# Two-part cache loads into any two free slots, and slots handed out in the order they came free

## The chip, the cores and the metric

The kernel runs on one core of one Trainium2 chip. Its time is the time on the device, in microseconds, of one execution; lower is better. The core has five engines with instruction streams of their own: TensorE (PE in the profile, its weight loads PEld), VectorE (DVE), ScalarE (ACT), GpSimd (POOL) and SyncE (SP). In this kernel SyncE issues the loads, and 16 DMA engines carry them out.

## The reference

The program is four layers for 8 sequences with one new token each: an attention layer A over cached keys and values, an MLP layer B, then A and B once more with the same weights and the same caches.

```python
def _A_ref(x, k_cache, v_cache, wq, wo):            # caches: 8 x 8 heads x 4096 x 256, bf16
    q = (x @ wq).reshape(B, Sq, 16, 256).transpose(0, 2, 1, 3)
    k = jnp.repeat(k_cache, 2, axis=1)
    v = jnp.repeat(v_cache, 2, axis=1)
    scores = jnp.einsum("bhqd,bhkd->bhqk", q, k) * (256 ** -0.5)
    p = softmax(scores)
    o = jnp.einsum("bhqk,bhkd->bhqd", p, v)
    return o.transpose(0, 2, 1, 3).reshape(B, Sq, 16 * 256) @ wo

def _B_ref(x, w1, w2, w3, w4):                      # one token: the shifted parts are zero
    ...
    x1 = x + hs
    return x1 + gelu(layernorm(x1) @ w3) @ w4

x = x + _A_ref(layernorm(x), A_k_cache, A_v_cache, A_wq, A_wo)
x = x + _B_ref(layernorm(x), B_w1, B_w2, B_w3, B_w4)
x = x + _A_ref(layernorm(x), A_k_cache, A_v_cache, A_wq, A_wo)
x = x + _B_ref(layernorm(x), B_w1, B_w2, B_w3, B_w4)
```

The four shifted pieces of `hs` move tokens by one or two places. With one token each of them is empty, so `hs` is zero and `w1` and `w2` don't matter. The large data are the two caches, read for both attention layers.

## The kernel before

A **unit** is one head of one sequence in one of the two attention passes, `(pass, sequence, head)`: 2 x 8 x 8 = 128 units. The keys and the values of a unit are 2 MiB each and are cut into four **parts** of 512 KiB. In each of 128 partitions a part is 4 KB, and the four parts of a partition are neighbours in memory: parts 0 and 1 together are one run of 8 KB per partition, and so are parts 2 and 3.

The parts live in 31 **slots** of 4 KB per partition, which are cut from one large tile, `slab` (L79, L80). A key part passes through two slots: it is loaded raw into one, VectorE transposes it into another (L554), and the raw slot is free again. TensorE uses the transposed keys for the scores (`k_part`, matmuls at L645). A value part is loaded into a slot and used where it lies (`v_part`, matmuls at L622). The transposed keys of six of the eight heads of a sequence stay in their slots from the first pass to the second (a few of these parts are parked in PSUM meanwhile and copied back at L512), so that they are loaded only once. Loaded are 832 parts.

The order of the work is written out by hand. The main loop (L784) goes over units, in four steps each. In a step come, among others, transposes for a part ahead, the scores of one part (`k_part`), the softmax pieces of the unit before, and the value parts planned for this step (`v_part`). Between the first and the second pass of a sequence lies the MLP, a chain of small steps on TensorE, VectorE and ScalarE (`mid_steps`); the loop fills it with units of other sequences. Below, this stretch is the layer change. `loads` is the list of all loads in the order in which they are to be issued.

The slots are managed in the same walk, on the host, when the program is made. `free` is the list of free slots. Each time the walk reaches an instruction that ends the use of a slot, the slot is put at the end of `free`, and `pump` (L502) issues as many loads as it can, always keeping one free slot back (`RESERVE`, L18), which a transpose can take as its destination (L550). On the chip, a load into a slot waits until the instruction that freed it has run; that wait follows from the slot that was chosen. SyncE issues the loads in order, each one behind the one before it, so a load that waits holds up those behind it. A load also waits for the one eight places before it, since eight completion semaphores go round.

`wide` (L453) holds the parts that may be loaded two at a time: those whose loads are planned outside the layer changes. For them `take_two` (L479) looks for an even slot and its neighbour, both free, and the load is one transfer of 1 MiB, one run of 8 KB per partition on both sides. If there is no such pair and at least `ENOUGH` = 7 parts are under way, `pump` stops and waits for a pair (L522); with fewer under way it loads one part. `take` (L472) prefers a slot whose neighbour is not free, so that pairs stay whole, and the lowest number among those. One part is a transfer of 512 KiB, one run of 4 KB per partition.

Of the kernel before, what the change touches and what calls it, by code (L numbers as in the profile page):

```python
# [15 lines left out]
UNIT = 2048  # L16
N_SLOTS = 31
RESERVE = 1  # L18
# [11 lines left out]
def kernel(  # L30
# [48 lines left out]
    slab = slotp.tile([128, N_SLOTS * UNIT], BF16, name="slab")  # L79
# [291 lines left out]
    lone = {b: [(1, b + 2, g) for g in loose] for b in range(4)}  # L371
# [31 lines left out]
    t = 0  # L403
    while t < n_units:
# [4 lines left out]
        p, b, g = units[t]  # L409
        n = 1  # L410
# [3 lines left out]
        for j in range(parts_):  # L414
            m = n // parts_ + (j < n % parts_)
# [26 lines left out]
    for t in order:  # L442
        for s in range(4):
            i = late_v.get((t, s), 4 * t + s + LAG)
            if t in ends or units[t + 1 : t + 2] == [GAP]:
                i = 4 * t + (6, 6, 7, 7)[s]
            elif t + 1 == n_units:
                i = 4 * t + (5, 5, 6, 7)[s]
# [7 lines left out]
    for i in range(4 * n_units + 8):  # L456
        n = len(loads)
# [6 lines left out]
        t, q = divmod(i + 2, 4)  # L464
# [3 lines left out]
    free = list(range(N_SLOTS))  # L468
# [2 lines left out]

    def take():  # L472

        lone = [x for x in free if x ^ 1 not in free]
        x = min(lone or free)
        free.remove(x)
        return x

    def take_two():  # L479

        both = [x for x in free if x % 2 == 0 and x + 1 in free]
        if both:
            free.remove(both[0])
            free.remove(both[0] + 1)
        return both[:1]

    extra = []
    for c in range(3):
# [13 lines left out]
    def pump():  # L502
        while loads and len(free) > RESERVE:
            kind, t, i = loads[-1]
            _, b, g = units[t]
            if kind == "p":
                loads.pop()
                x = take()
                dst = slots[x].rearrange("p (e q c x) -> p q c e x", e=4, q=2, c=4)
                for j in range(2):  # L510
                    src = park[parked[g, i]][j][:].bitcast(BF16)
                    nc.scalar.copy(dst[:, j], src.rearrange("p (c e x) -> p c e x", c=4, e=4))  # L512
                kt_of[(1, b, g), i] = x
                continue
            cache, of = (A_k_cache, raw_of) if kind == "k" else (A_v_cache, v_of)
            n, two = 1, (kind, t, i + 1)
            if i % 2 == 0 and two in wide and two in loads[-PAIR_VIEW:]:
                x = take_two() if len(free) > RESERVE + 1 else []
                if x:
                    n, x = 2, x[0]  # L520
                    loads.remove(two)
                elif under_way[0] >= ENOUGH:  # L522
                    return
            loads.pop()
            if n == 1:
                x = take()
            src = cache[b, g].rearrange("(p s e) d -> p s (e d)", s=4, e=8)
            nc.sync.dma_start(
                slab[:, UNIT * x : UNIT * (x + n)].rearrange("p (s d) -> p s d", s=n),
                src[:, i : i + n],  # L530
            )
            for m in range(n):
                of[t, i + m] = x + m
            under_way[0] += n
            n_loads[0] += n
            if n_loads[0] >= 8 and extra:
                nc.sync.dma_start(*extra.pop(0))
# [3 lines left out]
    def transposes(i):  # L541


        while len(parts) - len(todo) < by[i]:
            t, s = todo[-1]
            if 4 * t + s > i and ((t, s) not in raw_of or not free):
                return
            todo.pop()
            raw = raw_of.pop((t, s))
            kt = kt_of[units[t], s] = take()  # L550
            src = slots[raw].bitcast(FP32).rearrange("p (q c e i) -> p q c e i", q=2, c=4, e=4)
            dst = slots[kt].bitcast(FP32).rearrange("p (e q c r) -> p q c e r", e=4, q=2, c=4)
            for q in range(2):
                nc.vector.transpose(dst[:, q], src[:, q])  # L554
            _, b, g = units[t]
            if (g, s) in parked:
                for q in range(2):
                    dst = park[parked[g, s]][q][:].rearrange("p (c e r) -> p c e r", c=4, e=4)
                    nc.vector.transpose(dst, src[:, q])
            free.append(raw)  # L560
            under_way[0] -= 1
            pump()
# [49 lines left out]
    def v_part(t, s):  # L612
        if s == 0:
            at = PO + 4 * (nth[t] % n_po)
            pos[t] = pyb[:, at : at + 4].rearrange("p (k h) -> p k h", h=2)
            if nth[t] == n_po // 2:
                nc.vector.memset(pyb[:, PO : PO + 4 * (len(order) - n_po)], 0.0)
        v = v_of.pop((t, s))
        vv = slots[v].rearrange("p (c d) -> p c d", d=Dh)
        for c in range(8):  # L620
            for k in range(2):
                nc.tensor.matmul(  # L622
                    pos[t][:, k, :],
                    vv[:, c, 128 * k : 128 * k + 128],
                    pts[t][:, 8 * s + c, :],
                    start=(t == 0 and s == 0 and c == 0 and k == 0),
                    stop=True,
                    skip_group_check=True,
                )
        free.append(v)  # L630
        under_way[0] -= 1
        pump()

    def k_part(t, s):
        u = units[t]
        p, b, g = u
        if s == 0:
            assert t not in runs or t in ready
            scs[t] = scb[t % 2][:, 0:64].rearrange("p (c b h) -> p c b h", b=4, h=2)
        key = (u if fresh(u, s) else (1, b, g)), s  # L640
        ktv = slots[kt_of[key]].rearrange("p (e c m x) -> p e c m x", e=4, c=2, x=2)
        for c in range(2):
            for db in range(4):
                for x in range(2):
                    nc.tensor.matmul(  # L645
                        scs[t][:, 2 * s + c, :, :],
                        ktv[:, db, c, :, x],
                        Qblk[run_of[t][0]][:, run_of[t][1], db, x, :, :],
                        start=(db == 0 and x == 0),
                        stop=(db == 3 and x == 1),  # L650
                    )
        if p == 2 or g in loose or (g, s) in parked:
            free.append(kt_of.pop(key))
            pump()
# [129 lines left out]
    for t in range(n_units + 1):  # L784
        cur = t < n_units
        for q in range(4):
            i = 4 * t + q
# [152 lines left out]
```

## Time and profile before

| | before |
|---|---|
| median of 3 runs | 1124.85 us (1121.68 to 1127.41) |
| the profiled execution | 1124.39 us, span 1122.6 us |
| granted TensorE clock | 1.000 |
| read from HBM | 446.77 MB, 398 GB/s over the span |
| loads of two parts | 155 of values, 109 of keys |
| loads of one part | 202 of values, 102 of keys |
| from issue to landing, two parts | 12.6 us (values), 12.9 us (keys), median |
| from issue to landing, one part | 8.0 us (values), 8.6 us (keys), median |

The span runs from the first to the last instruction of the profiled execution; its own time is 1.8 us longer than its span. Where the profile cuts the span into 40 slices, one slice is 28 us. GB/s is what the DMA engines moved in a slice, and the DMA digits say how busy they were in tenths. In the lines on waits, an arrow points from who waited to what released it; the numbers are microseconds in total, how often, and the longest. SPq stands for SyncE's queue of DMA issues.

### The profile page before, as it was taken

How to read it: one execution, taken by the hardware profiler on the slowest of the kernel's cores; microseconds unless marked ns; L12 is line 12 of the kernel's file. 1: busy time of each engine (PE TensorE's matmuls, PEld its weight loads, DVE VectorE, ACT ScalarE, POOL GpSimd, SP SyncE). 2: the span in 40 equal slices, each digit the busy share in tenths (PEclk: the TensorE clock that was granted, in tenths of full speed). 3: DMA queues.
4: the chain of work that ended last, by engine and by line, in shares of the span. 5: the costliest groups of instructions: out<-in, count | busy, mean ns of one | idle time of the engine just before them, and what ended most of it. 6: DMA issues, size and time to landing. Idle time of an engine off the chain costs nothing. (4 is left out here: it accounts for less than half of the span.)

```text
span 1122.6 us, 46232 instructions
## 1 busy us (share of the span) xinstructions
PE 684.8 (61%) x20737; PEld 640.8 (57%) x20737; DVE 549.3 (49%) x1305; ACT 306.8 (27%) x1360; POOL 104.2 (9%) x156
## 2 busy tenths in 40 slices
PE   3345675666656575665756676666666665565765
PEld 2334564566646575655646565555656665565765
DVE  4347544644455445554546534653456425554322
ACT  1112223321332212421233222422243222421241
POOL 0000000100000000100001001000001000100101
DMA  9999999999999999999999999999999999999992
GB/s 366 396 419 425 405 409 424 423 418 389 392 425 423 411 402 420 424 423 395 418 403 424 412 412 388 425 423 413 363 417 424 422 402 374 424 422 411 363 403 93
DMA packets 89174, 449.76 MB, mean 401 GB/s; under 512 B 9344, under 2 KB 15376, under 8 KB 54800
## 3 DMA queue, kind: packets, MB, share of 16 engines
q1 hardware_dynamic: 88976, 446.81, 98.0%
q8 instruction: 162, 2.65, 0.8%
q14 instruction: 36, 0.29, 0.1%
HBM read 446.77 MB, written 0.01 MB: 398 GB/s over the span
## 5 line engine op out<-in xcount | busy, mean ns | idle before, releaser
L554 DVE STREAM_TRANSPOSE slab<-slab 128x512 f32<-128x512 f32 x640 | 413.4, 686 | 217.0 <-DMA slab<-in_A_k_cache_dram 158.1
L622 PEld LDWEIGHTS <-slab 128*128 128x128 bf16 x8192 | 273.5, 106 | 296.9 <-DMA slab<-in_A_v_cache_dram 245.5
L622 PE MATMUL bank<-pt,slab 128*128 128x2 bf16 x7168 | 259.9, 166 | 246.0 <-DMA slab<-in_A_v_cache_dram 174.7
L645 PE MATMUL bank<-Qblk,slab 128*128 128x8 bf16 x8192 | 296.9, 168 | 71.3 <-DVE slab L554 40.0
L645 PEld LDWEIGHTS <-slab 128*128 128x128 bf16 x8192 | 268.0, 105 | 78.7 <-DVE slab L554 47.4
L681 ACT ACTIVATE pe<-bank,small 128x32 bf16<-128x32 f32 x256 | 61.3, 296 | 417.1 <-DVE small L678 417.1
L723 POOL TENSOR_TENSOR small<-small 128x2 f32<-128x2 f32 x112 | 78.2, 698 | 794.1 <-DVE small L719 794.1
L712 ACT CAST pt<-bank 32x64 bf16<-32x64 f32 x448 | 91.1, 203 | 100.6 <-PE bank L704 96.1
L678 DVE TENSOR_REDUCE small<-bank 128x2 f32<-128x256 f32 x128 | 54.1, 423 | 103.3 <-PE bank L668 103.0
L719 DVE TENSOR_REDUCE small<-bank 128x2 f32<-128x64 f32 x128 | 27.2, 212 | 124.9 <-ACT pt L712 106.4
L164 ACT CAST Qblk<-bank 32x32 bf16<-32x32 f32 (+1 forms) x272 | 48.4, 178 | 121.2 <-PE bank L158 118.9
L668 PE MATMUL bank<-rows,small 128*128 128x128 bf16 x256 | 48.5, 293 | 19.0 <-DVE small L660 18.8
L660 DVE TENSOR_REDUCE small<-bank 128x2 bf16<-128x64 f32 x128 | 26.4, 206 | 59.6 <-PE bank L645 59.4
L622 PE MATMUL bank<-pt_far,slab 128*128 128x2 bf16 x1024 | 36.9, 166 | 25.0 <-DMA slab<-in_A_v_cache_dram 24.3
L704 PE MATMUL bank<-pe,rows 128*128 128x64 bf16 x512 | 51.2, 241 | 0.5 <-issue 0.5
L704 PEld LDWEIGHTS <-rows 128*128 128x128 bf16 x512 | 33.7, 124 | 27.8 <-issue 27.5
L694 PE MATMUL bank<-pe,small 128*128 128x64 bf16 x128 | 27.3, 213 | 33.4 <-ACT pe L681 32.0
L180 PEld LDWEIGHTS <-wo_sb 128*128 128x128 bf16 x1152 | 35.5, 104 | 8.6 <-issue 7.5
L180 PE MATMUL bank<-OT,wo_sb 128*128 128x1 bf16 x1024 | 33.2, 165 | 5.5 <-ACT OT L591 4.5
L135 PEld LDWEIGHTS <-wq_sb 128*128 128x128 bf16 x864 | 30.6, 106 | 9.2 <-issue 4.7
L512 ACT COPY slab<-park 128x1024 bf16<-128x1024 bf16 x32 | 30.4, 1024 | 8.2 <-DVE slab L554 6.1
L591 ACT ACTIVATE OT<-bank,small 128x2 bf16<-128x2 f32 x122 | 25.5, 261 | 23.9 <-PE bank L622 22.5
(113 smaller groups left out, 386.4 us busy)
## 6 DMA issues: line engine op xcount, KB each, us to landing
slab<-in_A_v_cache_dram SPq DMA_DIRECT2D x155, 1024.0 KB, 12.6
slab<-in_A_k_cache_dram SPq DMA_DIRECT2D x109, 1024.0 KB, 12.9
slab<-in_A_v_cache_dram SPq DMA_DIRECT2D x202, 512.0 KB, 8.0
slab<-in_A_k_cache_dram SPq DMA_DIRECT2D x102, 512.0 KB, 8.6
wo_sb<-in_A_wo_dram SPq DMA_DIRECT2D x4, 896.0 KB, 11.3
wq_sb<-in_A_wq_dram SPq DMA_DIRECT2D x3, 1024.0 KB, 6.8
w_sb<-in_B_w_dram SPq DMA_DIRECT2D x1, 1568.0 KB, 12.4
w_sb<-in_B_w_dram SPq DMA_DIRECT2D x3, 448.0 KB, 16.8
```

Source lines behind the costliest of these rows:

```text
L135: nc.tensor.matmul(pv[:, i, j, :], cols(big[:, c, :], m + i * half), rows[:, c, :], start=(i == 0 and j == 0 and c == 0), stop=True, skip_ ...
L164: nc.scalar.copy(dst, src)
L180: nc.tensor.matmul(y[:, c, :], chunk(wo_sb[:, k, :], c), o[:, k, :], start=False, stop=True, skip_group_check=True,)
L554: nc.vector.transpose(dst[:, q], src[:, q])
L622: nc.tensor.matmul(pos[t][:, k, :], vv[:, c, 128 * k : 128 * k + 128], pts[t][:, 8 * s + c, :], start=(t == 0 and s == 0 and c == 0 and k ...
L645: nc.tensor.matmul(scs[t][:, 2 * s + c, :, :], ktv[:, db, c, :, x], Qblk[run_of[t][0]][:, run_of[t][1], db, x, :, :], start=(db == 0 and x ...
L668: nc.tensor.matmul(mzs[t][:, 128 * h : 128 * h + 128], pm[:, h : h + 1].to_broadcast([128, 128]), ident, start=True, stop=True,)
L678: nc.vector.tensor_reduce(nm, mx, AX.X, ALU.max, negate=True)
L681: nc.scalar.activation(pe[:].rearrange("p c b h -> p h (c b)")[:, h], scs[t].rearrange("p c b h -> p h (c b)")[:, h], ACT.Exp, bias=nm[:, ...
L704: nc.tensor.matmul(pp[:, c], sel, pe[:], start=True, stop=True)
L712: nc.scalar.copy(pts[t][sl].rearrange("p (k c) h -> p k c h", c=4), pp[sl, :, :, pb, :].rearrange("p c k h -> p k c h"),)
L723: nc.gpsimd.tensor_tensor(out=rz_of[t], in0=zs, in1=mone, op=ALU.pow)
```

## The change

A load of two parts takes the two slots that have been free longest, whichever they are, in place of an even slot and its neighbour. The load's destination has three dimensions: partitions, the two slots with the step between them, and the 4 KB in a slot. Where the two slots happen to be neighbours, it is one run of 8 KB as before. `take` hands out the slot that has been free longest. The rule that `pump` stops when it gets no two slots and 7 parts are under way stays, and so does the reserve of one slot; what is loaded, in which order, and which loads may be of two parts is unchanged. Since slots are chosen differently, the points at which loads stand among the other instructions shift, and with them how many loads are of two parts: 297 in place of 264, with 238 of one part in place of 304.

```diff
     def take():
 
-        lone = [x for x in free if x ^ 1 not in free]
-        x = min(lone or free)
-        free.remove(x)
-        return x
+        return free.pop(0)
 
     def take_two():
 
-        both = [x for x in free if x % 2 == 0 and x + 1 in free]
-        if both:
-            free.remove(both[0])
-            free.remove(both[0] + 1)
-        return both[:1]
+        two = sorted(free[:2])
+        del free[:2]
+        return two
...
             if i % 2 == 0 and two in wide and two in loads[-PAIR_VIEW:]:
-                x = take_two() if len(free) > RESERVE + 1 else []
-                if x:
-                    n, x = 2, x[0]
+                xs = take_two() if len(free) > RESERVE + 1 else []
+                if xs:
+                    n = 2
                     loads.remove(two)
                 elif under_way[0] >= ENOUGH:
                     return
             loads.pop()
             if n == 1:
-                x = take()
+                xs = [take()]
             src = cache[b, g].rearrange("(p s e) d -> p s (e d)", s=4, e=8)
             nc.sync.dma_start(
-                slab[:, UNIT * x : UNIT * (x + n)].rearrange("p (s d) -> p s d", s=n),
+                slab.rearrange("p (x d) -> p x d", d=UNIT)[:, xs[0] : xs[-1] + 1 : max(xs[-1] - xs[0], 1)],
                 src[:, i : i + n],
             )
             for m in range(n):
-                of[t, i + m] = x + m
+                of[t, i + m] = xs[m]
```

## The prediction

> **What bounds the kernel now.** I read the page from the top: busy times, the forty slices, the DMA queues.
>
> ```profile
> PE 684.8 (61%) x20737; PEld 640.8 (57%) x20737; DVE 549.3 (49%) x1305; ACT 306.8 (27%) x1360; POOL 104.2 (9%) x156
> ...
> DMA  9999999999999999999999999999999999999992
> GB/s 366 396 419 425 405 409 424 423 418 389 392 425 423 411 402 420 424 423 395 418 403 424 412 412 388 425 423 413 363 417 424 422 402 374 424 422 411 363 403 93
> ...
> q1 hardware_dynamic: 88976, 446.81, 98.0%
> ```
>
> No engine is above 61%. The 16 DMA engines are busy at 98%, and the bytes are fixed by the problem. So two things can move the time: how fast a busy DMA engine moves bytes, and how often it has nothing to do. The GB/s line shows both: stretches at 424, and dips to 363.
>
> For the first I asked for the DMA view of two stretches of 20 us: 340 to 360, where only two-part loads run, and 650 to 670, where only one-part loads run. First 340 to 360, then 650 to 670:
>
> ```profile
> DMA packets 1162, 8.48 MB, mean 424 GB/s; under 512 B 130, under 2 KB 130, under 8 KB 130
> ...
> q1 hardware_dynamic: 1158, 8.42, 100.2%
> ```
> ```profile
> DMA packets 2273, 8.31 MB, mean 415 GB/s; under 512 B 252, under 2 KB 252, under 8 KB 2270
> ...
> q1 hardware_dynamic: 2270, 8.27, 101.7%
> ```
>
> Both stretches are full. A two-part load into neighbouring slots is one run of 8 KB in each partition and travels as 8 KB packets; a one-part load travels as 4 KB packets. Each queue packet under 512 B is the end mark of a load. So 1158 - 130 = 1028 packets of 8 KB took 20 us x 16 engines, 311 ns each; 2270 - 252 = 2018 packets of 4 KB took 158.6 ns each, 317.1 ns for a pair.
>
> For the second, the stretches in which the DMA moves clearly less (columns: stretch, length, busy time of the five engines with instruction counts, granted clock, DMA share, GB/s):
>
> ```profile
> 240.00:280.00 40.00, 25.42 (x760) 23.71 (x760) 18.68 (x55) 6.90 (x33) 3.21 (x5) 1.00 1.01 395
> 300.00:320.00 20.00, 10.15 (x311) 9.03 (x309) 8.05 (x17) 5.95 (x22) 1.39 (x2) 1.00 1.01 396
> 380.00:400.00 20.00, 12.30 (x357) 11.65 (x354) 6.95 (x20) 4.49 (x22) 1.40 (x2) 1.00 1.01 390
> 500.00:540.00 40.00, 26.11 (x812) 24.62 (x810) 17.83 (x48) 8.09 (x39) 2.79 (x4) 1.00 1.00 402
> 560.00:580.00 20.00, 11.69 (x354) 10.76 (x354) 10.37 (x22) 5.89 (x30) 2.10 (x3) 1.00 1.02 396
> 640.00:660.00 20.00, 12.03 (x380) 11.31 (x376) 6.90 (x17) 4.49 (x22) 1.40 (x2) 1.00 1.01 397
> 680.00:700.00 20.00, 11.12 (x350) 10.54 (x346) 10.39 (x22) 4.86 (x24) 1.40 (x2) 1.00 0.99 376
> 780.00:820.00 40.00, 26.72 (x824) 25.59 (x825) 16.61 (x51) 8.19 (x39) 3.34 (x5) 1.00 0.98 373
> 920.00:940.00 20.00, 13.74 (x437) 13.24 (x435) 9.28 (x21) 6.11 (x30) 1.95 (x3) 1.00 0.97 349
> ```
>
> Against the 415 of full 4 KB traffic they lack, as length x (1 - GB/s / 415): 1.9, 0.9, 1.2, 1.3, 0.9, 0.9, 1.9, 4.0 and 3.2 us, 16.2 us in all. They lie around the change from one layer to the next, where most slots hold keys that wait for the second pass.
>
> What the loads wait for there is in SyncE's own waits:
>
> ```profile
> SPq L528 <- PE bank L622: 241.9, 187, 5.3
> SPq L528 <- DVE slab L554: 162.9, 75, 5.9
> ```
>
> L622 (a V part's matmuls) and L554 (a transpose) are what frees slots: the loads queue behind the freeing of slots.
>
> Last, the chain of waits at its end (start, length, what):
>
> ```profile
> 1021.67 8.09 DMA slab<-in_A_v_cache_dram
> ...
> 1032.87 4.68 DMA slab<-in_A_v_cache_dram
> 1037.63 0.54 issue
> ...
> 1108.35 0.86 PE bank L622 x32
> ```
>
> Up to 1037 us the end waits for loads. After that, 85 us of matmuls, softmax and MLP follow with no load in the chain: a faster or slower DMA there changes nothing.
>
> **The change, term by term.** The profiled execution took 1124.39 us (span 1122.6), 0.46 below the median of 1124.85; I add to 1124.4.
>
> 1. *Smaller packets.* Counted in the two built programs: before, 264 two-part loads, all in neighbouring slots, and 304 of one part; after, 297 of two parts, of which 36 happen to get neighbouring slots, and 238 of one. The 261 others have two runs of 4 KB in each partition. Slab packets before: 128 x (264 + 304) = 72,704. After: 128 x (36 + 238) + 256 x 261 = 101,888. That is 29,184 more, 1,824 on each engine. A load written in two separate runs is not in the trace; the nearest row is the stretch at 650, where a pair of 4 KB packets took 317.1 - 311.3 = 5.9 ns longer than one of 8 KB: 10.8 us. Low end: that stretch also has 122 more end marks, which a two-part load wouldn't; at their recorded 9 ns (packet records) they are 0.34% of it, which leaves 4.8 ns and 8.8 us. High end: the packet records themselves, 159 and 309 ns, so 9 ns and 16.4 us. I take 10.8, a sustained rate, since the recorded durations of neighbouring packets overlap (share 101.7%). Of the 264 two-part loads, 15 are issued after 1037 us, where the chain has no load: x 0.94 gives **+10.2 us** (8.2 to 15.4). No cover hides it: the DMA is full.
>
> The Trainium skill, "DMA: Bandwidth & Descriptors", Specifications, gives 512 B as the smallest transfer for line rate; by that, 4 KB and 8 KB pieces are equally fast and this term is zero. The trace disagrees: 415 against 424 GB/s in two full stretches. The same page (Why small descriptors are slow) speaks of about 3 cycles of overhead per packet; at the 850 MHz that it gives for the fabric that is an estimate of 3.5 ns, 6.4 us for the 1,824 packets.
>
> 2. *Fewer loads.* 33 fewer issues and end marks: 33 x 9 ns = 0.3 us on each engine, left out. An issue with more runs can cost SyncE more (L537: 984 ns median for the 1,024 runs of a wo load, 328 ns for a plain one); at 256 runs an estimate of 0.5 us. SyncE spends over 700 us waiting for slots, so this is hidden except behind an empty queue.
>
> 3. *Loads wait for an older slot.* One free slot is always kept back. Counted in the order that the planner writes out: before, 435 of 568 loads write a slot freed by the very event that let the load be issued (78 of 125 in the layer changes); after, 15 of 535 (0 of 119), since the oldest free slot goes first and the kept one is the newest. So a load is ready one freeing earlier, as if one more part were queued. Where the DMA is full this buys nothing. In a dip it fills up to one part's time, 524,288 B at 415 GB/s = 1.26 us. Capped so, the nine dips give 1.26 + 0.9 + 1.2 + 1.26 + 0.9 + 0.9 + 1.26 + 1.26 + 1.26 = 10.2 us, times 78/125 = **-6.3 us**. Ends: 0, if what empties the queue is that nothing is freed for longer; -16.2, if the dips vanish. I take the capped sum: it follows from one slot.
>
> 4. *No holding out for neighbours.* Before, up to 8 slots lie free while a load waits for a pair (2.5 free on average after a load, 1.4 after the change). This happens outside the layer changes, where the stretch at 340 is full anyway: 0. Just behind a layer change it may add to term 3, within its end.
>
> 5. *A new wait on VectorE.* The slot kept back is what a transpose takes as its destination. Before, 51 of 256 transposed parts took one that a V part's matmuls (L622) had just freed; after, 194. VectorE then waits for TensorE, and behind the transpose are queued its softmax maxima, sums and MLP steps, for which TensorE and ScalarE wait. Nearest row:
>
> ```profile
> DVE slab L554 <- PE bank L622: 11.3, 8, 2.8
> ```
>
> 11.3 us over 51 such parts is 0.22 us a part; 143 more make 32 us. VectorE is idle for half the span, so it counts only near the dips: the nine stretches are 240 of 1037 us, 7.3 us; even there the DMA lacks only 16 of 240 us. Ends 0 and 7.3; I take **+2 us**, nearer to zero for that reason.
>
> Sum: 1124.4 + 10.2 - 6.3 + 2 = 1130.3, so **1130 us**, 0.5% above the median.
>
> **Rivals.**
> - *The dips were the whole price.* One more queued part, and the slots no longer held out for pairs behind the layer changes, close all dips (-16.2), term 5 stays 0 and term 1 is at its low end: 1124.4 + 8.2 - 16.2 = 1116 us, faster. For it: SyncE's 163 us behind transposes. Against it: the deepest dips (4.0 and 3.2 us) are longer than one part. It decides once terms 3 and 5 together return over 15.4 us against 10.2.
> - *The wait moves to VectorE.* If each of the 143 new waits lasts the 1.4 us that the 8 seen ones last, they are 202 us, 23% of it in the dips' stretches, 46 us; if a quarter reaches the DMA, +11.6 in place of +2: 1140 us. For it: at a layer change TensorE and VectorE already wait for one another. Against it: TensorE is idle for 39% and usually done early.
> - *Splitting is free* (a two-run load travels like an 8 KB one; the skill's 512 B rule points that way): 1124.4 - 6.3 + 2 = 1120 us. Against it: the two full stretches.
>
> **How the numbers follow.** About 0.5% (1119.2 to 1130.5) is what a measurement of this kernel can tell from no change. The forecast case has 0.58; its ends put 0.28 within 0.5% and 0.30 above. The first rival has 0.17 (faster), the second 0.17 (slower), free splitting 0.08 (0.05 same, 0.03 faster). So faster 0.20, same 0.33, slower 0.47. The range must take in 1116 and 1140 but for 2 in 10: 1118 to 1141, the top also for term 1 at 15.4 without any refund (1142). The forecast's own range is 1124 to 1138.
>
> **What would show it.** Term 1: packets under 8 KB rise by 58,368 (128 x 238 + 256 x 261 - 128 x 304) less some 500 end marks, to about 112,600, packets of 8 KB fall to about 5,000, and full stretches run at 415 to 418 where they ran at 424. If full stretches stay at 424, splitting is free. Term 3: SyncE's waits for L622 and L554 shrink, and the nine dips are shallower by about 1 us each; unchanged dips prove it wrong. Term 5: VectorE's wait for L622 at the transposes rises from 11 us to some 40; far above 100 speaks for the second rival. The tail behind the last load in the chain stays near 85 us; if it changes by several us, my split at 1037 us is wrong.

## The result, and the profile after

The changed kernel takes 1919.75 us (median, 1917.46 to 1927.82) against 1123.26 us before: 1.71 times as long, 95% interval 1.7044 to 1.7155. The forecast was 1130 us. The loss is 796 us, nearly eighty times the largest single term that I had worked out.

The first lines of the page after (busy times, the slices, the packets, the DMA queue):

```profile
PE 683.5 (36%) x20737; PEld 645.1 (34%) x20737; DVE 552.6 (29%) x1305; ACT 306.8 (16%) x1360; POOL 104.4 (5%) x156
...
DMA  9745965668655785557965487646765586545962
GB/s 378 282 133 167 352 252 199 219 239 336 242 176 177 263 333 197 177 177 252 348 230 183 155 337 280 221 156 233 299 215 202 189 344 236 198 154 191 360 243 68
DMA packets 117831, 449.77 MB, mean 235 GB/s; under 512 B 8816, under 2 KB 14848, under 8 KB 112640
...
q1 hardware_dynamic: 117632, 446.81, 64.9%
```

The engines do the same work as before, and the packets are the ones forecast: 112,640 under 8 KB (forecast about 112,600) and 5,191 larger ones. But the DMA engines, busy at 98% before, are busy at 65%. No packet became slower: in the packet records a 4 KB packet took 159 ns before and after. Between the packets the DMA engines now stand idle. The dips are no longer the layer changes: the stretches with two-part loads, 424 GB/s before, are the slow ones, most of them at 133 to 250, and the layer changes, where loads have one part, stand out at 330 to 360.

What stands still shows best at the score matmuls. They read transposed keys, which VectorE writes, not a load. This is what ended TensorE's idle time (matmuls and weight loads) ahead of them, first before (L645), then after (the same line, now L640); columns: us in total, times.

```profile
  DVE slab L554: 87.4, 123
  issue: 54.2, 54
```
```profile
  DMA slab<-in_A_v_cache_dram: 924.4, 157
  DMA slab<-in_A_k_cache_dram: 553.9, 92
  issue: 342.0, 55
  DVE slab L549: 186.4, 90
```

Before, no idle time ahead of a score matmul was ended by a load. After, most of it is, and mostly by loads of *values*, which the scores never read. (Matmuls and weight loads wait side by side, so these sums count much of the time twice; ahead of the matmuls alone TensorE stood idle for 996 us.) The transposes, which read keys, wait for loads of values too, first before, then after:

```profile
DVE slab L554 <- DMA slab<-in_A_v_cache_dram: 3.8, 2, 2.1
```
```profile
DVE slab L549 <- DMA slab<-in_A_v_cache_dram: 224.4, 43, 9.4
```

A piece of the timeline after shows the rhythm (start, length, engine, line, what; in brackets the idle time before it and who ended it):

```profile
164.17 0.57 PE L640 MATMUL bank<-Qblk,slab 128*128 128x8 bf16 x16 [4.68 <-DMA slab<-in_A_k_cache_dram]
...
166.71 0.37 SPq L523 DMA_DIRECT2D slab<-in_A_v_cache_dram  x1
171.93 0.51 PEld L640 LDWEIGHTS <-slab 128*128 128x128 bf16 x16 [6.64 <-issue]
171.96 0.57 PE L640 MATMUL bank<-Qblk,slab 128*128 128x8 bf16 x16 [6.59 <-DMA slab<-in_A_v_cache_dram]
...
172.56 0.37 SPq L523 DMA_DIRECT2D slab<-in_A_k_cache_dram  x1
...
177.67 2.65 DVE L549 STREAM_TRANSPOSE slab<-slab 128x512 f32<-128x512 f32 x4 [3.65 <-DMA slab<-in_A_k_cache_dram]
...
177.71 0.57 PE L640 MATMUL bank<-Qblk,slab 128*128 128x8 bf16 x16 [4.49 <-DMA slab<-in_A_k_cache_dram]
...
180.38 0.37 SPq L523 DMA_DIRECT2D slab<-in_A_v_cache_dram  x1
```

One load of 1 MiB is issued, it lands about 5 us later, the score matmuls and transposes that waited for it run, and only then is the next one issued. Here the loads have lost their queue. The waits of SyncE and the time to landing say the same:

```profile
SPq L523 <- DVE slab L549: 1034.8, 219, 13.9
SPq L523 <- PE bank L617: 145.1, 102, 9.2
```
```profile
slab<-in_A_v_cache_dram SPq DMA_DIRECT2D x169, 1024.0 KB, 5.5
slab<-in_A_k_cache_dram SPq DMA_DIRECT2D x128, 1024.0 KB, 5.6
```

A two-part load lands in 5.5 us, where it took 12.6 in the full queue before: the load itself is not slow, it is alone. The issues at 166.7, 172.6 and 180.4 us make two loads of 1 MiB in 13.7 us, 153 GB/s.

The waits of the built program say why. I took each wait of an engine for a load and compared the slots that the load writes with those that the waiting instruction uses. Before, every such wait is for a load that writes one of them. After, 232 waits of the score matmuls and 235 of the transposes, 467 in all, are for a load that writes none of the slots in use, and in each of them a slot in use lies between the two slots of the load. The other way there are fewer: 33 loads wait for an instruction of TensorE or VectorE that uses none of their slots, but one between them. So SyncE waits for a transpose nearly always on account of the load's own slot, and the transpose is late because it waits for an earlier load. The waits are set when the program is made, and by these counts a load written with a step is taken there to write the whole stretch from its first slot to its last.

### The profile page after: what moved, and what is told of

It is laid out like the page before. It is cut to its first block, busy times and chain, and to the rows that moved or that the text cites. A ratio compares the mean times of both kernels' runs of the same rounds, so it can differ in the third digit from the quotient of the medians.

```text
span 1915.4 us, 46423 instructions
## 1 busy us (share of the span) xinstructions
PE 683.5 (36%) x20737; PEld 645.1 (34%) x20737; DVE 552.6 (29%) x1305; ACT 306.8 (16%) x1360; POOL 104.4 (5%) x156
## 2 busy tenths in 40 slices
DMA packets 117831, 449.77 MB, mean 235 GB/s; under 512 B 8816, under 2 KB 14848, under 8 KB 112640
## 5 line engine op out<-in xcount | busy, mean ns | idle before, releaser
L640 PE MATMUL bank<-Qblk,slab 128*128 128x8 bf16 x8192 | 295.6, 168 | 996.4 <-DMA slab<-in_A_v_cache_dram 544.9
L640 PEld LDWEIGHTS <-slab 128*128 128x128 bf16 x8192 | 264.7, 105 | 1015.0 <-DMA slab<-in_A_v_cache_dram 379.5
L663 PEld LDWEIGHTS <-small 128*128 128x128 bf16 x256 | 16.8, 106 | 56.8 <-DVE small L655 56.4
```

Of the source, the lines that this page charges most:

```text
L640: nc.tensor.matmul(scs[t][:, 2 * s + c, :, :], ktv[:, db, c, :, x], Qblk[run_of[t][0]][:, run_of[t][1], db, x, :, :], start=(db == 0 and x ...
L663: nc.tensor.matmul(mzs[t][:, 128 * h : 128 * h + 128], pm[:, h : h + 1].to_broadcast([128, 128]), ident, start=True, stop=True,)
```

## The experiments

**Theory 1, false waits:** whatever uses a slot between the two slots of a load waits for that load, and the load for it. **Theory 2, the order of handing out:** transposes get the newest slot and wait for TensorE (the second rival of the prediction). **Theory 3:** a load with a step is slow in the DMA engines.

### Two loads in place of one with a step

The changed kernel with this edit:

```diff
-            nc.sync.dma_start(
-                slab.rearrange("p (x d) -> p x d", d=UNIT)[:, xs[0] : xs[-1] + 1 : max(xs[-1] - xs[0], 1)],
-                src[:, i : i + n],
-            )
+            if xs[-1] - xs[0] > 1:
+                for m in range(2):
+                    nc.sync.dma_start(slots[xs[m]], src[:, i + m])
+            else:
+                nc.sync.dma_start(
+                    slab[:, UNIT * xs[0] : UNIT * (xs[0] + n)].rearrange("p (s d) -> p s d", s=n),
+                    src[:, i : i + n],
+                )
```

> The slots, their order and the order of the work are those of the changed kernel; only, a load of two parts whose slots are not neighbours is issued as two loads of one part, so that no load has a step (36 loads of two parts in neighbouring slots stay, 760 loads of one part). Theory 1, false waits: a load with a step is taken to write everything from its first slot to its last, so what uses the slots between waits for it, and it for them. Then nearly all of the 800 us goes: 1115 to 1145 us (before, plus up to 16 us for 4 KB packets, less up to 10 for older slots). Theory 2, the order in which slots are handed out (transposes get the newest slot and wait for TensorE): it stays above 1800 us. Theory 3, a load with a step is slow in the DMA engines: 1115 to 1145 us as well, with the loads landing as fast as plain ones; the run with gapped pairs tells 1 from 3.

Measured: 1125.84 us against 1125.07, ratio 1.0011 (1.0000 to 1.0022). The slots, their order and the order of the work are those of the changed kernel, and the whole loss is gone. Theory 2 falls. In its program no wait of an engine is for a load that doesn't write a slot in use.

### Pairs with an unused gap

With the 31st slot given up for room, an unused gap is put between the two slots of each pair. The slots, the order and the waits stay; only each two-part load has a step, with nothing used in between. The control is the kernel before with `N_SLOTS = 30`.

```diff
-    slab = slotp.tile([128, N_SLOTS * UNIT], BF16, name="slab")
-    slots = [slab[:, UNIT * i : UNIT * i + UNIT] for i in range(N_SLOTS)]
+    slab = slotp.tile([128, N_SLOTS * UNIT + (N_SLOTS // 2 + 1) * GAP_COLS], BF16, name="slab")
+    at_of = [UNIT * i + (i + 1) // 2 * GAP_COLS for i in range(N_SLOTS)]
+    slots = [slab[:, a : a + UNIT] for a in at_of]
...
-                slab[:, UNIT * x : UNIT * (x + n)].rearrange("p (s d) -> p s d", s=n),
-                src[:, i : i + n],
+                slots[x]
+                if n == 1
+                else slab[:, at_of[x] : at_of[x] + 2 * (UNIT + GAP_COLS)].rearrange(
+                    "p (s d) -> p s d", s=2
+                )[:, :, 0:UNIT],
+                src[:, i] if n == 1 else src[:, i : i + 2],
```

> The kernel before with 30 slots in place of 31: the control for the run with gapped pairs, which needs the room. One slot less means one part less in flight around the layer changes; by the prediction's third term this costs about what one more slot would give back, up to 10 us: 1123 to 1140 us.

> The control with 30 slots and an unused gap of 32 bytes between the two slots of each pair: the same slots, order and waits, but each of the 246 loads of two parts is written in two separate runs of 4 KB, with nothing that is used between them. Theory 1: no false waits, so only the packet term is left, 246 x 8 packets on each engine at 5 to 9 ns: 10 to 18 us above the control. Theory 3: the load with a step is slow in itself, hundreds of us above the control.

> As the run with gapped pairs (30 slots, 246 loads of two parts in two runs each), but the unused gap is 256 bytes in place of 32, so that every slot starts at a multiple of 256 bytes, as in the kernel before. The 32-byte gap cost 28 us, of which the packet term explains 10 to 18. If the rest came from the shifted starts of the slots (a quarter of the 4 KB packets took 164 ns or more there, 159 in the other runs), this run is 5 to 18 us above the control with 30 slots: 1130 to 1144 us, packets at 159 ns and full stretches at 415 GB/s or more. If it came from the load with a step as such, it stays at 1148 to 1156 us.

Measured: the control 1125.45 us (1.0006, 0.9991 to 1.0021), so one slot less costs nothing that can be told. With a gap of 32 bytes (`GAP_COLS = 16`) 1153.67 us (1.0252, 1.0226 to 1.0277), with 256 bytes (`GAP_COLS = 128`) 1135.57 us (1.0086, 1.0066 to 1.0106). The GB/s in the slices, first with 32, then with 256 bytes:

```profile
GB/s 353 386 407 410 381 409 410 410 404 374 403 410 409 397 380 391 409 410 389 405 401 410 410 393 385 412 408 399 389 407 408 407 382 377 408 407 391 357 411 94
```
```profile
GB/s 354 391 411 419 386 417 417 418 412 386 414 417 417 403 394 417 418 417 390 408 408 418 418 396 368 417 417 416 392 415 418 418 384 391 417 417 391 382 417 87
```

A full stretch moves 417 where two-part loads with a step run over a gap of 256 bytes, against 424 for neighbours. So 246 loads with a step and no false waits cost 1135.57 - 1125.45 = 10.1 us, the packet term. (The two ran on different chips; by their ratios to the kernel before, 1.0086 and 1.0006, it is 9.0 us.) Theory 3 falls: steps cost about 10 us, not 800. These steps span 4 KB and a gap, and in the changed kernel two slots lie up to 27 others apart, but its 4 KB packets took the same 159 ns. The first gap cost 28 us, outside its expected 10 to 18. The other 18 us belong to the shifted slots; more on that at the end.

### One slot between, and the nearest two of three

The kernel before, with pairs made of a slot and the next but one:

```diff
-        lone = [x for x in free if x ^ 1 not in free]
+        lone = [x for x in free if x ^ 2 not in free]
...
-        both = [x for x in free if x % 2 == 0 and x + 1 in free]
+        both = [x for x in free if x % 4 < 2 and x + 2 in free]
...
-                slab[:, UNIT * x : UNIT * (x + n)].rearrange("p (s d) -> p s d", s=n),
+                slab.rearrange("p (x d) -> p x d", d=UNIT)[:, x : x + 2 * n - 1 : 2],
```

> The kernel before with its own handing out, but a pair is a slot and the next but one, so each of its 256 loads of two parts has a step and exactly one slot lies between its two. In the program, 97 waits of other engines then name a load that does not touch the slots they use (in the changed kernel 467, in the kernel before none). Theory 1: a clear loss but a fraction of the 800 us; in proportion to these waits 800 x 97 / 467 = 165 us, 1290 us, range 1160 to 1450. Theory 2: no loss beyond the packets, 1123 to 1145 us. Theory 3: 256 of 261 such loads are there, so about the whole loss, 1800 us or more.

Measured: 1395.39 us (1.2407, 1.2382 to 1.2431). Its handing out is that of before, and one slot between two is enough for 270 us, inside the range that was expected of theory 1. What held up its score matmuls (L645), as above:

```profile
  DMA slab<-in_A_v_cache_dram: 349.8, 48
  DVE slab L554: 157.6, 102
  DMA slab<-in_A_k_cache_dram: 59.5, 8
```

The loads are there again as releasers, for 409 us in place of 1478. The changed kernel with less distance between the two slots:

```diff
-        two = sorted(free[:2])
-        del free[:2]
-        return two
+        two = min(((a, b) for a in free[:3] for b in free[:3] if a < b), key=lambda p: p[1] - p[0])
+        for x in two:
+            free.remove(x)
+        return list(two)
```

> The changed kernel, but a load of two parts takes those two of the three slots longest free that lie nearest to each other (lone slots by age as before; 91 loads get neighbours, 206 have a step). Counted in the program, 282 waits of the score matmuls and the transposes name a load that writes none of the slots they use; counted alike, the changed kernel has 467 and the run with one slot between 153 (the number 97 in that run's expectation left out 57 at the transposes). If the loss goes with these waits, 796 us x 282 / 467 = 481 us: 1600 us, range 1480 to 1720. If it goes with the number of loads with a step (206 against 261 and 256), 1750 or, by the run with one slot between, 1340.

Measured: 1483.5 us (1.3165, 1.3122 to 1.3208), at the low end of the expected range. Here is the row of the three kernels with steps over used slots, counted alike:

| kernel | loads with a step | false waits | above before |
|---|---|---|---|
| one slot between | 256 | 153 | 270 us |
| nearest two of three | 206 | 282 | 358 us |
| the changed kernel | 261 | 467 | 796 us |

The loss goes up with the false waits and not with the number of loads with a step. It is not in proportion: 1.8, 1.3 and 1.7 us a wait, with the some 10 us of the smaller packets still in each loss. Which waits cost more than others stays open.

### What is left: packets and the order by age

The kernel before with each two-part load issued as two of one part, in the same slots:

```diff
-            nc.sync.dma_start(
-                slab[:, UNIT * x : UNIT * (x + n)].rearrange("p (s d) -> p s d", s=n),
-                src[:, i : i + n],
-            )
+            for m in range(n):
+                nc.sync.dma_start(slots[x + m], src[:, i + m])
```

> The kernel before with the same slots in the same order, but each load of two parts issued as two loads of one part: all slab packets are 4 KB (832 loads). All theories expect no large loss; this measures the packet term of the prediction with the doubled end marks in it: 264 x 8 = 2112 more data packets on each engine at 5 to 9 ns and 264 more end marks at 6 to 9 ns, 12 to 21 us, of which 0.94 counts: 1134 to 1143 us. If it stays within 3 us of before, the packet term of the prediction was wrong.

Measured: 1134.13 us (1.0086, 1.0070 to 1.0102), 9.1 us above before and at the low end of what was expected. So the run with two loads in place of one (1125.84), which splits 228 pairs more than before against 264 here, has won about 7 us back. By what? First, lone slots by age in the kernel before:

```diff
-        x = min(lone or free)
+        x = (lone or free)[0]
```

> The kernel before, with pairs of neighbours as before, but a lone slot is handed out by age (the one that has been free longest among those without a free neighbour) and not by number. No load has a step. Theory 1 and 3: no large loss; with the refund of the prediction's third term up to 6 us faster, 1117 to 1126 us. Theory 2 (order by age costs): clearly slower, 1200 us or more.

Measured: 1124.15 us, 0.9994 (0.9979 to 1.0009): no gain. Yet in the layer changes only 1 of its 127 loads still writes a slot freed by the event that let it be issued (78 of 125 before). Then the run with two loads in place of one, with the newest slots handed out in place of the oldest:

```diff
-        return free.pop(0)
+        return free.pop()
...
-        two = sorted(free[:2])
-        del free[:2]
+        two = sorted(free[-2:])
+        del free[-2:]
```

> As the run with two loads in place of one (no step, loads of two parts split unless neighbours, no holding out for neighbours), but the newest free slots are handed out first in place of the oldest. Every one of the 535 loads or pairs then writes a slot freed by the event that let it be issued (15 there), at the same points of the program. That run won back about 7 us of the packet term. If this came from older slots, it is gone here: 1131 to 1137 us, and the dips around the layer changes lack about 16 us as before. If it came from not holding out for neighbours, this run is at 1124 to 1129 us.

Measured: 1133.56 us (1.0074, 1.0050 to 1.0098): the 7 us are gone. The loads and their points in the program are the same, but for nine more pairs that are split (27 neighbours against 36), 0.3 us at the rate above. The stretch from 40 to 1040 us of the oldest-first and of the newest-first kernel (columns as in the prediction):

```profile
40.00:1040.00 1000.00, 626.85 (x18649) 578.34 (x18650) 507.32 (x1163) 273.33 (x1233) 91.04 (x132) 1.00 1.02 411
```
```profile
40.00:1040.00 1000.00, 621.80 (x18502) 572.70 (x18499) 505.55 (x1152) 273.73 (x1235) 91.07 (x132) 1.00 1.02 408
```

411 against 408 GB/s is the same 0.7%. The difference lies in the dips. In stretches of 20 us from 20 to 1100 us, what is lacking to 417 GB/s adds up to 19 us with the oldest slots first, to 27 with the newest first, to 27 where the kernel before issues two loads for each pair, to 28 with lone slots alone by age, and to 26 in the kernel before. So older slots bring the gain, and lone slots alone do not. It comes mostly just behind the layer changes: from 160 to 180 us the first three moved 417, 358 and 387 GB/s, from 940 to 960 us 417, 369 and 387. Inside a layer change the dips are no shallower: from 380 to 400 us 384, 391 and 405. The two profiled executions are 10.5 us apart, and some 3 us of that have another cause: in the first 20 us the newest-first run moved 273 against 334 GB/s, since its first loads go to slots 27 to 30, which the setup is still using (one of them waits 9.3 us for TensorE there).

### Versions without steps that keep 8 KB runs and older slots

Neighbours if any two of the free slots but the newest are neighbours (one 8 KB run); else, if more than 4 or 5 slots are free, the two oldest by two loads; lone slots by age. From the run with two loads in place of one:

```diff
-    def take_two():
+    def take_two(must=False):
 
+        for a in free[:-1]:
+            for b in (a - 1, a + 1):
+                if b in free[:-1]:
+                    free.remove(a)
+                    free.remove(b)
+                    return sorted((a, b))
+        if not must:
+            return []
         two = sorted(free[:2])
...
-                xs = take_two() if len(free) > RESERVE + 1 else []
+                xs = take_two(len(free) > 5) if len(free) > RESERVE + 1 else []
```

> A candidate without steps: any two neighbouring slots among the free ones but the newest make a load of 8 KB runs (148 loads); if there are none and more than 4 slots are free, the two oldest are loaded by two loads of one part (122 times); lone slots go by age. It should keep the refund of the run with two loads in place of one (about 7 us) and lose about half of its packet term: 1117 to 1124 us. If the refund came from not holding out for neighbours, it shrinks with the larger number of free slots, and the time stays at 1123 to 1127.

> The same with more than 5 free slots before two slots that are not neighbours are taken: 214 loads of 8 KB runs, 51 split pairs. Packet term about 2 us, refund as far as it comes from older slots: 1116 to 1123 us; without it 1123 to 1127.

Measured: 1122.33 us (0.9977, 0.9965 to 0.9988) with 4 and 1122.22 us (0.9977, 0.9963 to 0.9990) with 5, against 1124.94. Both are faster than the kernel before, by 0.1 to 0.4%, and can't be told from each other. Most full stretches are back at 420 to 424, as the slices of the version with 5 show:

```profile
GB/s 366 398 420 424 408 417 424 423 405 403 417 423 422 395 399 420 423 422 385 417 417 419 424 393 396 423 423 415 397 405 424 419 410 386 422 424 396 394 423 51
```

## Why the prediction was wrong

**The step that failed** stands ahead of all five terms: that a load waits for what last used its own two slots, and that only users of these two wait for it. It is in the description of the kernel (the wait "follows from the slot that was chosen"), and term 3 ("a load is ready one freeing earlier, as if one more part were queued") is where it entered the sum. A wait for slots that a load does not touch had no term, so it was put at nothing. In the changed program score matmuls and transposes wait 467 times for a load that only has their slot between its two, which have up to 27 slots between them, and 33 loads wait in the same way. The loads behind then wait for slots that these matmuls and transposes free. Where two-part loads run, the queue of loads, on which the full DMA rests, became a queue of about one; that cost the 796 us. No rival had this: all three moved the known terms about. The waits stand in the built program; comparing their targets with the slots in use would have shown 467 of them where the kernel before has none. I had looked at which *engines* the loads wait for and at the ages of the slots that the planner hands out, and taken the waits to follow from that.

**Term 1, packets: the right mechanism, the size a little high.** The packet counts came out as forecast, and 4 KB packets still took 159 ns. I took 10.2 us for 228 more split pairs (8.2 to 15.4). The loads with a step over a 256-byte gap cost 9.0 to 10.1 us for 246 pairs, 8.3 to 9.4 for 228; two plain loads in their place 9.1 us for 264 pairs with their end marks, 7.8 for 228. By that, splitting is not free: full stretches of 4 KB pieces ran at 417 against 424 GB/s. The Trainium skill ("DMA: Bandwidth & Descriptors", Specifications) has transfers at line rate from 512 B on; here a difference of some 2% is left between 4 and 8 KB. The estimate from its 3 cycles a packet (Why small descriptors are slow; 3.5 ns) gives 6.5 us for 246 pairs (246 x 8 x 3.5 ns x 0.94), against 9.0 to 10.1 measured. The factor 0.94 was not borne out: the last load in the chain that ended last landed 37 us before the end in the changed kernel and 25 us before it in the run with two loads in place of one, not 85.

**Term 2, fewer loads:** an issue of a load with a step took 0.37 us, where some 0.5 had been taken; no run shows a cost of it.

**Term 3, older slots: about the right size, by luck in part.** I took -6.3 us, summed from the nine dips and scaled by the one-part loads in the layer changes. Oldest against newest first is worth 1133.56 - 1125.84 = 7.7 us, about 5 without the slow start of the newest-first run. But by age for lone slots alone, which are the ones in the layer changes, it is worth nothing (0.9994); what was won lies mostly just behind them.

**Term 4, no holding out: small, not measured by itself.** The newest-first run does not hold out for neighbours either and stays 0.74% above before, 8 us, about what its packets cost. Since some 3 us of that lie in its start, a gain of that size from not holding out is not ruled out.

**Term 5, VectorE's new wait: right in the wait, the cost not seen.** Forecast was that VectorE's wait for value matmuls rises from 11 us to some 40. In the run with two loads in place of one, which hands slots out as the changed kernel does, it is

```profile
DVE slab L553 <- PE bank L621: 52.0, 40, 3.0
```

Yet that run is the faster one of the two orders, and in the newest-first run the same wait is 16.1 us. A cost of 2 us was not seen; the runs can't tell one so small.

Without the false waits the forecast would have stood: 1125.84 us, inside its range and 4 us below 1130, with terms 1 and 3 each about right and nearly cancelling. **Rivals:** none of them happened. The second had the right sign and, with theory 2, the wrong cause: the same handing out without steps costs 0.1%.

## What to carry to other kernels

Before a strided or multi-part access replaces a contiguous one, compare the waits of the built program: for every wait, whether what it waits for touches what the waiting instruction uses. A stepped write into a shared tile can be taken for its whole stretch, and a kernel that lives on loads in flight pays for such false waits with its queue; here two plain transfers in place of each one with a step took away the whole 796 us. In a trace the sign is an engine released by a transfer whose data it never reads, together with a time to landing that goes *down*.

## What the runs showed of the hardware that was not expected

The start of the slots matters. With the gap of 32 bytes the run took 1153.67 us, with 256 bytes 1135.57, at the same slots, order and number of packets; full stretches ran at 410 against 417 GB/s, one-part loads included. In the packet records a quarter of the 4 KB packets took 164 ns or more with the 32-byte gap, and 159 at the same quartile with 256. The Trainium skill, "DMA: Bandwidth & Descriptors", How a descriptor splits into AXI transactions, says that a transaction must start at a multiple of 256 bytes, and that a descriptor which starts elsewhere begins at the boundary below, so that bytes before its start are fetched for nothing. The runs agree in sign, but the page speaks of fetched bytes and here it is the side written that is shifted, so the cause is not shown. Gaps between 32 and 256 bytes weren't tried.

One slot of 31 less cost nothing that can be told (1.0006, 0.9991 to 1.0021), though by the third term's reasoning it takes one part out of the queue around each layer change.
